# One list schedule for both feed-forwards of an attention and two-feed-forward kernel, with measured lengths and dependent operations kept apart

## The chip, the cores and the metric

The kernel runs on one core of a Trainium2 chip. The time is the device time of one execution in microseconds (us). Three runs of the kernel before took 731.81, 727.86 and 728.3 us; their median is 728.3 us. The execution that was profiled took 728.8 us, and the span that its trace covers is 726.7 us.

Five engines take part. PE (TensorE) multiplies matrices, and PEld is its loading of weights, which runs beside it. DVE (VectorE) and ACT (ScalarE) do the work between the products. POOL (GpSimd) squares one tensor of each chunk. SP issues every DMA.

## The reference

Three stages follow one another on 2304 tokens (4 sequences of 576) with 512 features:

```python
# attention, 8 heads of 64, each row sees itself and the 63 rows before it
scores = (q @ k.T) / 8, masked to 0 <= row - col < 64
x = softmax(scores) @ v                       # [2304, 512]
# feed-forward 1
h = maximum(x @ w_in, 0)                      # [2304, 2048]
x2 = (h * h) @ w_out                          # [2304, 512]
# feed-forward 2
h = x2 @ w2_in                                # [2304, 1024]
solu = h * softmax(h)                         # over the 1024
ln = (solu - mean) / sqrt(var + 1e-6) * g_ln  # over the 1024
out = ln @ w2_out                             # [2304, 512]
```

The two weight matrices of each feed-forward come as 64-bit floating point numbers.

## The kernel before, in words

**Blocks, units and passes.** The rows are cut into 36 blocks of 64. Two blocks make a unit of the attention: one call of `attention(n, rank)`, in which PE forms the scores, DVE masks them and takes the maxima, ACT takes the exponentials, POOL scales, PE transposes, ACT copies, PE multiplies with v, and ACT and DVE split the result into two parts, `x`. Feed-forward 1 runs over the blocks in five passes of 8, 6, 8, 6 and 8 blocks (`PASSES`), so of 512, 384, 512, 384 and 512 columns.

**Products in three terms.** Each product of a feed-forward is the sum of three (`TERMS`): high part by high part, high by low, low by high. A 128-row chunk of the hidden layer (`kk`, 16 in feed-forward 1) is then one group of 12 matmuls into `ps_h` (`product`, L402) and one of 12 into `ps_y` (`second`, L428). Between the two, ACT takes the relu and the square, POOL the exact square, and DVE the rest that the high part leaves (`rest`, L418).

**Weights.** `weights()` turns a 128x512 piece from 64-bit numbers into a high and a low part: ACT scales (L206), DVE shifts and masks (`bits`, L210), puts in the sign (`sign`, L215) and the low bits (`low`, L220), ACT rounds (`first`, L228) and DVE takes the rest (`second`, L231). The three DVE operations in the middle write and read one tile, `wm`. Feed-forward 1 has 32 such pieces (16 `wa`, 16 `wb`), all made in pass 0, and feed-forward 2 has 16 (`w2i`, `w2o`), made in the last pass in the room that used `wa` pieces leave. For this reason pass 0 goes twice over the chunks, with two halves of 256 columns: the second half starts `BEHIND` = 6 chunks after the first.

**The order of the work.** Attention, feed-forward 1 and the weights are tasks of a `Plan`. Each task has an engine, an expected length, a rank, its predecessors and the buffers that it takes and gives. `Plan.run` is a list scheduler: again and again it takes the task that could start first, with the lower rank where two could start at once. A result costs `HOP` = 0.12 us more if it goes to another engine and nothing if it stays. Tasks marked `port` on DVE and POOL don't overlap in the plan. The instructions are then issued in that order, and every engine works through its own list strictly in order.

**Feed-forward 2 before** is no part of the plan. It is written out by hand behind it, from L527, in 18 tiles of 128 rows: `load_x` reads x2 back from DRAM, `split_x` splits it, `mm_h` (L547) makes `ps_h` with 24 matmuls of 512 columns and then runs the softmax and the statistics on DVE and ACT, `mm_t` transposes (`ps_lt`, L587), `mm_o` makes `ps_o` with 24 matmuls and stores. Its `ps_h` uses the PSUM pair of buffers `b` that also holds the four sums `ps_y` of feed-forward 1.

Of the kernel before, what the change touches and what calls it, by code (L numbers as in the profile page):

```python
# [8 lines left out]
F32 = mybir.dt.float32  # L9
# [9 lines left out]
P = 128  # L19
# [5 lines left out]
class Plan:  # L25
# [6 lines left out]
    HOP = 0.12  # L32
# [10 lines left out]
    def run(self):  # L43
# [6 lines left out]
        while any(todo.values()):  # L50
            best = None
            for eng, ts in todo.items():
                for t in ts:
# [3 lines left out]
                    for a in t["after"]:  # L57
                        at = max(at, a["end"] + (self.HOP if a["eng"] != eng else 0.0))
# [35 lines left out]
def kernel(  # L94
# [33 lines left out]
    HALF, BEHIND = len(FIRSTS), 6  # L128
# [32 lines left out]
    x2_dram = dram.tile([P, DC, NT], F32, name="x2_dram")  # L161
# [12 lines left out]

    with ExitStack() as c1:
# [3 lines left out]
        g_p = c1.enter_context(tc.tile_pool(name="g", bufs=3))  # L179
        ps_t = c1.enter_context(tc.tile_pool(name="ps_t", bufs=2, space=PSUM))  # L180
# [9 lines left out]
        plan = Plan({"raw": RAWS, "wm": WMB, "qk": 1, "v": 1, "e": 2, "pt": 1, "t": 2, "b": 2, "a": 2, "r": 2, "g": 3})  # L190
# [5 lines left out]
        def weights(kind, i, rank, after=()):  # L196
# [37 lines left out]
            a = add("SP", 1.9, rank - 9, load, after, take=["raw"], late=2.0)  # L234
            b = add("ACT", 0.60, rank, scale, [a], take=["wm"])
            c = add("DVE", 0.37, rank, bits, [b], port=True)
            c = add("DVE", 0.62, rank, sign, [c], port=True)
            c = add("DVE", 0.62, rank, low, [c], port=True, give=["raw"])
            b = add("ACT", 0.60 + 0.66 * (kind == "2o"), rank, first, [c])
            ready[kind, i] = add("DVE", 0.62, rank, second, [b], port=True, give=["wm"])  # L240
# [6 lines left out]
        def attention(n, rank):  # L247
# [26 lines left out]
            def load_v():  # L274
                o["v"] = vt = at_p.tile([P, 2, DM], F32, tag="v", name="vt", bufs=1)
# [90 lines left out]
            qk = ["r", "r"] if n == 1 else ["qk"]  # L366
            lq = add("SP", 1.9, rank - 6, load_qk, take=qk, late=2.0)
            lv = add("SP", 1.0 * half, rank - 2, load_v, [v_after.get(n - 1)], take=["v"], late=2.0)
            v_after[n] = lv
            s = add("PE", 0.5 + 0.45 * half, rank, scores, [lq], take=["t", "t", "e"], give=qk)  # L370
            first_scores.append(s)
            ns = []
            for a in range(2):
                d = add("DVE", 0.05 + 0.3 * half, rank, lambda a=a: masked(a), [s], give=["t"])
                d = add("DVE", 0.05 + 0.3 * half, rank, lambda a=a: maximum(a), [d])
                for b in range(0, HP, HP // 2):
                    e = add("ACT", 1.0 + 0.07 * half, rank, lambda a=a, b=b: exps(a, b), [d])
                d = add("DVE", 0.32, rank, lambda a=a: inverse(a), [e])
                ns.append(add("POOL", 0.12 + 0.48 * half, rank, lambda a=a: norm(a), [d], port=True))
            p = add("PE", 0.12 + 0.43 * half, rank, transposes, [*ns, p_after.get(n - 1)], take=["t"] * half + ["pt"], give=["e"])  # L380
            c = [add("ACT", 0.58, rank, lambda a=a: copied(a), [p], give=["t"]) for a in range(half)]
            p = add("PE", 1.35, rank, values, [*c, lv], take=["b" if alone else "t"], give=["pt", "v"])
            p_after[n] = p
            h = add("ACT", 0.62, rank, high, [p] + x_free.get(t - 2, []))
            x_ready[n] = add("DVE", 0.65, rank, rest, [h], give=["b" if alone else "t"])


        acc, in_of, out_of = {}, {}, {}

        def mm(N):  # L390
            return 12 * (N / 2400 + 0.0125) + 0.05

        def ffn(t, n0, n1, kk, rank, done):
# [28 lines left out]
            def second():  # L422
                if t not in acc:
                    acc[t] = [ps_b.tile([P, 2, 512], F32, tag="b", name="ps_y") for _ in range(2)]
                for d in range(DC):
                    for n, (wi, xi) in enumerate(TERMS):

                        T.matmul(acc[t][d // 2][:, d % 2, n0:n1], wb[kk][:, wi, d * P : d * P + P], o["g"][:, xi, :N],  # L428
                                 start=kk == 0 and n == 0 and n0 == 0, stop=last and n == 2)

            i = add("PE", mm(N), rank, product, [ready["a", kk], *done], take=["a"])
# [3 lines left out]
            r = add("ACT", N / 1200 + 0.14, rank, relu, [i], take=["r"], give=["a"])  # L435
            s = add("ACT", N / 1200 + 0.16, rank, square, [r], take=["g"])
            e = add("POOL", N / 550 + 0.13, rank, exact, [s], port=True)
            e = add("DVE", N / 960 + 0.1, rank, rest, [e], port=True, give=["r"])
            first = kk == 0 and n0 == 0
            before = out_of.get((t, 0, 0)) if kk == 0 else out_of[t, n0, kk - 1]  # L440
            p = add("PE", mm(N), rank + 4.5, second, [e, ready["b", kk], before], take=["b", "b"] if first else [], give=["g"])
            out_of[t, n0, kk] = p
            if last:
                ys = []
                for d in range(DC):
                    def evict(d=d):
                        o["y", d] = y = raw_p.tile([P, 512], F32, tag="wm", name="y", bufs=WMB)
                        if d % 2:
                            S.activation(out=y[:, :n1], in_=acc[t][d // 2][:, d % 2, :n1], func=AF.Copy)  # L449
                        else:  # L450
                            V.tensor_copy(y[:, :n1], acc[t][d // 2][:, d % 2, :n1])

                    def store(d=d):
                        at = starts[t] * BLK
                        nc.sync.dma_start(out=x2_dram[:, d, at : at + n1], in_=o["y", d][:, :n1])

                    y = add("ACT" if d % 2 else "DVE", 0.62, rank, evict, [p] + ys[-1:] * (d % 2), take=["wm"], give=["b"] * (d % 2))
                    ys.append(y)
                    add("SP", 1.0, rank, store, [y], late=2.0, give=["wm"])


        PAIR0, PAIR = 13.0, 6.6
# [8 lines left out]
        for n in range(u0):  # L471
            attention(n, 2.0 + n)
        for i in range(u0):
            attention(u0 + i, begin[0] + i * (BEHIND - 1) * PAIR / u0)

        def attention_of(t):
            lo = begin[t - 1] + (BEHIND * PAIR if t == 1 else 0)
# [47 lines left out]


    with ExitStack() as c2:  # L527
        s_p = c2.enter_context(tc.tile_pool(name="s", bufs=2))
        ps_t = c2.enter_context(tc.tile_pool(name="ps_t2", bufs=2, space=PSUM))
        NTT = NT // P  # L530
        sol, lnT, rst = {}, {}, {}
        x2 = {}

        def load_x(i):
            xr = s_p.tile([P, DC, P], F32, tag="xr", name="xr")
            nc.sync.dma_start(out=xr, in_=x2_dram[:, :, i * P : i * P + P])
            x2[i] = xr

        x2s = {}

        def split_x(i):
            xr = x2.pop(i)
            xx = s_p.tile([P, 2, DC, P], F32R, tag="xx", name="xx")
            S.activation(out=xx[:, 0], in_=xr, func=AF.Copy)
            V.tensor_tensor(out=xx[:, 1], in0=xr, in1=xx[:, 0].bitcast(F32), op=ALU.subtract)
            x2s[i] = xx

        def mm_h(i):
            xx = x2s.pop(i)
            ps = ps_b.tile([P, 2, 512], F32, tag="b", name="ps_h2")  # L550
            for hf in range(NH2):
                n = 0
                for c in range(DC):
                    for wi, xi in TERMS:
                        T.matmul(ps[:, hf, :], xx[:, xi, c, :], w2i[hf * DC + c][:, wi, :],  # L555
                                 start=n == 0, stop=n == 3 * DC - 1)
                        n += 1
            h = ps.rearrange("p a b -> p (a b)")
            nmax = s_p.tile([P, 1], F32, tag="nmax2", name="nmax2")
            V.tensor_reduce(out=nmax, in_=h, axis=AX.X, op=ALU.max, negate=True)  # L560
# [12 lines left out]
            rstd = s_p.tile([P, 1], F32, tag="rstd", name="rstd", bufs=4)
            V.tensor_scalar(out=rstd, in0=mv[:, 1:2], scalar1=1e-6, scalar2=None, op0=ALU.add)  # L574
# [86 lines left out]
```

## Time and profile before

| | |
|---|---|
| median of 3 runs | 728.3 us |
| profiled execution, its span | 728.8 us, 726.7 us |
| PE busy | 697.0 us (96%) |
| PEld, DVE, ACT, POOL busy | 605.5, 371.5, 307.9, 139.0 us |
| chain that ended last | PE 81%, DVE 11%, issue 2%, DMA 2%, ACT 2% |

The busy shares are averages over stages that differ. In the first 140 us DVE makes the weights; after that PE works without a break until the end of feed-forward 1; then comes a short gap, and feed-forward 2 is again PE without a break. How the span falls into stages is read from the windows, and what ended the chain in each of them from the chain of waits.

### The profile page before, as it was taken

The numbers are of one execution on the slowest core, as the hardware profiler recorded it, in microseconds if no ns is written. First come the engines' busy times: TensorE is split into PE (matmuls) and PEld (weight loads), VectorE is DVE, ScalarE is ACT, GpSimd is POOL, SyncE is SP. The second block draws the span as 40 slices with busy tenths as digits, with TensorE's granted clock in tenths as the row PEclk, the third lists the DMA queues.
The fourth block names the chain that finished last, engine by engine and source line by source line (L and its number), as shares of the span: only waits on it lengthen the run. The fifth ranks groups of instructions, "written<-read, shape, count | busy, mean of one in ns | idle before, by whom it ended". The sixth has DMA issues, their size and how long they took to land.

```text
span 726.7 us, 11758 instructions
## 1 busy us (share of the span) xinstructions
PE 697.0 (96%) x4630; PEld 605.5 (83%) x4630; DVE 371.5 (51%) x678; ACT 307.9 (42%) x755; POOL 139.0 (19%) x161
## 2 busy tenths in 40 slices
PE   6687999999999999999999999998999999999997
PEld 3677888999999888788999988886888888888876
DVE  3999999522333221322223166555675646665561
ACT  5776767334445233433434243455323231323132
POOL 2122332412223122222222121121010011010100
PEclk9889999999999999999999999999999999999999
DMA  7766644012222211212111062222211011110001
GB/s 225 252 203 227 212 151 147 31 38 87 66 66 67 73 36 30 63 40 86 39 66 60 1 206 99 89 85 66 80 44 58 30 45 44 59 39 35 14 30 43
DMA packets 34565, 60.51 MB, mean 83 GB/s; under 512 B 5072, under 2 KB 16336, under 8 KB 34512
## 3 DMA queue, kind: packets, MB, share of 16 engines
q1 hardware_dynamic: 34512, 59.78, 24.7%
q8 instruction: 36, 0.59, 0.3%
q14 instruction: 17, 0.14, 0.1%
HBM read 50.34 MB, written 9.44 MB: 82 GB/s over the span
## 4 chain that ended last, share of the span: by engine, by line
PE 81%; DVE 11%; issue 2%; DMA 2%; ACT 2%; SPq 0%; POOL 0%; ACTq 0%; DVEq 0%
PE ps_h L402 24%; PE ps_y L428 23%; PE ps_h L555 14%; PE ps_o L599 14%; DVE wm L215 3%; PE ps_lt L587 2%; DVE wm L220 2%; PE ps_v L350 2%; PE ps_s L294 2%; PE ps_p L327 1%; DVE wm L210 1%; DVE wa L231 1%; DVE g L418 1%; DVE wb L231 1%; DMA qk<-in_k 1%
## 5 line engine op out<-in xcount | busy, mean ns | idle before, releaser
L402 PE MATMUL ps_h<-x,wa 128*128 128x256 f32 (+2 forms) x1152 | 220.5, 344 | 4.3 <-DVE wa L231 2.5
L428 PE MATMUL ps_y<-g,wb 128*128 128x256 f32 (+2 forms) x1152 | 219.6, 343 | 5.2 <-DVE g L418 5.0
L428 PEld LDWEIGHTS ps_y<-g,wb 128*128 128x128 f32 x1152 | 188.2, 190 | 26.2 <-DVE g L418 7.1
L402 PEld LDWEIGHTS ps_h<-x,wa 128*128 128x128 f32 x1152 | 190.4, 194 | 23.1 <-DVE wa L231 3.4
L415 POOL TENSOR_TENSOR r<-r 128x256 f32<-128x256 f32 (+2 forms) x96 | 84.0, 877 | 305.3 <-ACT g L412 288.3
L418 DVE TENSOR_TENSOR g<-r,g 128x256 fp32r<-128x256 f32 (+2 forms) x96 | 55.0, 580 | 152.0 <-POOL r L415 147.6
L408 ACT ACTIVATE r<-ps_h 128x256 f32<-128x256 f32 (+2 forms) x96 | 46.9, 489 | 157.6 <-PE ps_h L402 153.4
L555 PE MATMUL ps_h<-w2i,xx 128*128 128x512 f32 x432 | 104.9, 393 | 0.4 <-ACT y L449 0.4
L599 PE MATMUL ps_o<-w2o,lnT 128*128 128x512 f32 x432 | 104.5, 391 | 0.8 <-ACT lnT L588 0.5
L599 PEld LDWEIGHTS ps_o<-w2o,lnT 128*128 128x128 f32 x432 | 80.7, 188 | 17.9 <-ACT lnT L588 0.8
L555 PEld LDWEIGHTS ps_h<-w2i,xx 128*128 128x128 f32 x432 | 79.9, 188 | 17.0 <-ACT y L449 0.8
L309 ACT ACTIVATE e<-e,nmax 128x128 f32<-128x128 f32 (+1 forms) x144 | 55.0, 384 | 38.4 <-DVE nmax L305 38.4
L602 ACT ACTIVATE o<-ps_o,rstd 128x512 f32<-128x512 f32 x18 | 12.4, 689 | 111.8 <-PE ps_o L599 109.9
L575 POOL TENSOR_TENSOR rstd<-rstd,mhalf 128x1 f32<-128x1 f32 x18 | 16.8, 935 | 192.5 <-DVE rstd L574 192.5
L412 ACT ACTIVATE g<-r 128x256 fp32r<-128x256 f32 (+2 forms) x96 | 50.3, 524 | 5.1 <-PE ps_y L428 2.3
L318 POOL TENSOR_TENSOR e<-e,sums 128x512 f32<-128x512 f32 (+1 forms) x36 | 37.0, 1031 | 73.2 <-DVE sums L315 61.9
L560 DVE TENSOR_REDUCE nmax<-ps_h 128x1 f32<-128x1024 f32 x18 | 21.9, 1218 | 43.9 <-PE ps_h L555 43.9
L301 DVE SCALAR_TENSOR_TENSOR e<-ps_s,mask 128x512 f32<-128x512 f32 (+1 forms) x36 | 23.5, 653 | 38.9 <-PE ps_s L294 38.9
L589 DVE TENSOR_TENSOR lnT<-ps_lt,lnT 128x512 fp32r<-128x512 f32 x36 | 23.3, 683 | 36.3 <-ACT lnT L588 36.3
L220 DVE SCALAR_TENSOR_TENSOR wm<-wraw,wm 128x512 int32<-128x512 int32 x48 | 36.3, 757 | 1.2
L215 DVE SCALAR_TENSOR_TENSOR wm<-wraw,wm 128x512 int32<-128x512 int32 x48 | 35.1, 731 | 1.3
L206 ACT ACTIVATE wm<-wraw 128x512 f32<-128x512 f32 x48 | 31.5, 664 | 2.3 <-DMA wraw<-in_w_out 1.7
(57 smaller groups left out, 511.9 us busy)
## 6 DMA issues: line engine op xcount, KB each, us to landing
wraw<-in_w_in SPq DMA_DIRECT2D x24, 512.0 KB, 3.8
wraw<-in_w_out SPq DMA_DIRECT2D x24, 512.0 KB, 3.3
vt<-in_v SPq DMA_DIRECT2D x32, 256.0 KB, 2.9
kt<-in_k SPq DMA_DIRECT2D x16, 384.0 KB, 4.2
xr<-x_dram SPq DMA_DIRECT2D x18, 256.0 KB, 3.1
out<-o SPq DMA_DIRECT2D x18, 256.0 KB, 2.0
qt<-in_q SPq DMA_DIRECT2D x17, 256.0 KB, 2.8
x_dram<-y SPq DMA_DIRECT2D x12, 256.0 KB, 2.5
```

The lines of the kernel that those rows point to most:

```text
L215: V.scalar_tensor_tensor(out=t, in0=o["raw"][:, :, 1], scalar=-0x80000000, in1=t, op0=ALU.bitwise_and, op1=ALU.bitwise_or)
L220: V.scalar_tensor_tensor(out=t, in0=o["raw"][:, :, 0], scalar=29, in1=t, op0=ALU.logical_shift_right, op1=ALU.bitwise_or)
L309: S.activation(out=o["er"][:, a, w], in_=o["er"][:, a, w], func=AF.Exp, bias=o["nmax"][:, a, w : w + 1], accum_out=o["sums"][:, a, w : w + 1])
L318: G.tensor_tensor(out=o["er"][:, a], in0=o["er"][:, a], in1=o["sums"][:, a].unsqueeze(2).to_broadcast([P, HP, W]), op=ALU.mult)
L402: T.matmul(ps[:, :N], wa[kk][:, wi, c * P : c * P + P], xs[t][:, xi, c, n0:n1], start=n == 0, stop=n == 3 * DC - 1)
L408: S.activation(out=o["r"], in_=o["h"][:, :N], func=AF.Relu)
L412: S.activation(out=o["g"][:, 0, :N], in_=o["r"], func=AF.Square)
L415: G.tensor_tensor(out=o["r"], in0=o["r"], in1=o["r"], op=ALU.mult)
L418: V.tensor_tensor(out=o["g"][:, 1, :N], in0=o["r"], in1=o["g"][:, 0, :N].bitcast(F32), op=ALU.subtract)
L428: T.matmul(acc[t][d // 2][:, d % 2, n0:n1], wb[kk][:, wi, d * P : d * P + P], o["g"][:, xi, :N], start=kk == 0 and n == 0 and n0 == 0, sto ...
L555: T.matmul(ps[:, hf, :], xx[:, xi, c, :], w2i[hf * DC + c][:, wi, :], start=n == 0, stop=n == 3 * DC - 1)
L599: T.matmul(ps, l[:, xi, kk, :], w2o[kk][:, wi, :], start=n == 0, stop=n == 3 * KF2 - 1)
```

## The change

1. **Both feed-forwards are in the plan.** The hand-written part goes. A function `tile2` adds the steps of each tile of feed-forward 2 as tasks. The products with `w2i` are two tasks of 12 matmuls, those with `w2o` also two; the transposes of a tile are placed 6 us of rank behind its products, and the `w2o` products 1.5 tiles behind (growing to 3.9 over the last four tiles). Its working tiles lie in the room of used `wb` pieces. In the last pass the four sums `ps_y` take one buffer of the pair `b` and the two single buffers `t` of the attention, so that the other `b` is free for the first tile of feed-forward 2. x2 goes to five DRAM tensors, one for each pass, so that a read waits for its own pass alone. The last chunk's product of the last pass gets a rank 6 us earlier.
2. **Dependent operations stay apart.** A result that stays on its engine now costs `GAP` = 0.1 us on DVE and ACT, and the hop depends on the engine that gives it (0.10 to 0.35 us).
3. **Lengths.** Nearly all expected lengths are changed (a weight load from 1.9 to 1.4 us, a square on POOL of 256 columns from 0.60 to 0.62 us, two exponentials of a late unit from 1.14 to 0.77 us, and so on).
4. **Pass 0.** `BEHIND` is 2 and not 6; the ranks of the units and chunks are new. The second unit's v goes into a free `g` buffer instead of waiting for the single buffer `v`.

```diff
-    HOP = 0.12
+    HOP = {"DVE": 0.16, "ACT": 0.14, "POOL": 0.35, "PE": 0.12, "SP": 0.1}
+    GAP = {"DVE": 0.1, "ACT": 0.1}
...
-                        at = max(at, a["end"] + (self.HOP if a["eng"] != eng else 0.0))
+                        at = max(at, a["end"] + (self.HOP[a["eng"]] if a["eng"] != eng else self.GAP.get(eng, 0.0)))
...
-    HALF, BEHIND = len(FIRSTS), 6
+    HALF, BEHIND, LAST = len(FIRSTS), 2, len(PASSES) - 1
...
+                if n == 1:
+                    o["v"] = vt = g_p.tile([P, 2, NMAX], F32, tag="g", name="vt")
...
-                    acc[t] = [ps_b.tile([P, 2, 512], F32, tag="b", name="ps_y") for _ in range(2)]
+                    acc[t] = [ps_b.tile([P, 2, 512], F32, tag="b", name="ps_y") for _ in range(1 if t == LAST else 2)]
+                    acc[t] = [a[:, i] for a in acc[t] for i in range(2)]
+                    if t == LAST:
+                        acc[t] += [ps_t.tile([P, 512], F32, tag="t", name="ps_y") for _ in range(2)]
...
-        PAIR0, PAIR = 13.0, 6.6
+        PAIR0, PAIR = 14.29, 8.64
+        V0, LATER, OUT = -2.75, 40.72, 4.28
+        UNIT = (1.43, 3.36, 23.15, 34.53)
...
+            a = add("SP", 1.0, rank - 14, load_x, stored[t] + h_of.get(i - 3, []), take=["wb"], late=2.0)
+            a = add("ACT", 0.54, rank - 6, x_high, [a], take=["wb"])
+            a = add("DVE", 0.60, rank - 6, x_low, [a], port=True, give=["wb"])
+            for hf in range(NH2):
+                a = add("PE", mm(512), rank, lambda hf=hf: mm_h(hf), [a, *(ready["2i", hf * DC + c] for c in range(DC))],
+                        take=["b"] * (hf == 0), give=["wb"] * (hf == 1))
+            h_of[i] = [a]
+            a = add("DVE", 1.17, rank, max_h, [a])
+            a = add("ACT", 1.10, rank, exp_h, [a], take=["wb"])
+            a = add("DVE", 1.60, rank, solu, [a], give=["b"])
+            a = add("DVE", 1.50, rank, stats, [a])
+            r = add("POOL", 1.05, rank, root, [a])
+            a = add("DVE", 0.56, rank, centered, [a], port=True)
+            p = add("PE", 0.95, rank + 6, transposes2, [a], take=["t", "t"], give=["wb"])
...
+        NTT, TILE = NT // P, 4 * mm(512) + 1.2
+        for i in range(NTT):
+            at = begin[-1] + TILE * i
+            tile2(i, at, at + TILE * (1.5 + 0.6 * max(0, i - (NTT - 5))))
```

**DVE in pass 0.** The numbers tell the tiles apart: `wm` is the piece under work. Before:

```order
L210 TENSOR_SCALAR wm_1291<-wm_1291 128x512
L215 SCALAR_TENSOR_TENSOR wm_1291<-wraw_1245,wm_1291 128x512
L220 SCALAR_TENSOR_TENSOR wm_1291<-wraw_1245,wm_1291 128x512
L210 TENSOR_SCALAR wm_1330<-wm_1330 128x512
L215 SCALAR_TENSOR_TENSOR wm_1330<-wraw_1270,wm_1330 128x512
L220 SCALAR_TENSOR_TENSOR wm_1330<-wraw_1270,wm_1330 128x512
L231 TENSOR_TENSOR wa_1441<-wm_1291,wa_1441 128x512
```

And in the changed kernel, where L212, L217, L222, L233 and L424 are the former L210, L215, L220, L231 and L418:

```order
L217 SCALAR_TENSOR_TENSOR wm_909<-wraw_844,wm_909 128x512
L233 TENSOR_TENSOR wa_1025<-wm_881,wa_1025 128x512
L222 SCALAR_TENSOR_TENSOR wm_909<-wraw_844,wm_909 128x512
L424 TENSOR_TENSOR g_1031<-r_1029,g_1031 128x256
L217 SCALAR_TENSOR_TENSOR wm_952<-wraw_887,wm_952 128x512
L212 TENSOR_SCALAR wm_1010<-wm_1010 128x512
L233 TENSOR_TENSOR wb_1067<-wm_909,wb_1067 128x512
L222 SCALAR_TENSOR_TENSOR wm_952<-wraw_887,wm_952 128x512
L233 TENSOR_TENSOR wa_1096<-wm_952,wa_1096 128x512
```

An operation on a piece now mostly has one on another tile between itself and the operation that it needs.

**PE between the feed-forwards.** `ps_y` is feed-forward 1; `ps_h` with a number is a tile of feed-forward 2. Before:

```order
L402 MATMUL ps_h<-x,wa 128x512 x12
L428 MATMUL ps_y<-g,wb 128x512 x24
L555 MATMUL ps_h_5103<-w2i,xx 128x512 x24
L555 MATMUL ps_h_5151<-w2i,xx 128x512 x24
```

And in the changed kernel (L408, L437 and L543 are the former L402, L428 and L555):

```order
L408 MATMUL ps_h<-x,wa 128x512 x12
L437 MATMUL ps_y<-g,wb 128x512 x12
L543 MATMUL ps_h_5073<-w2i,xx 128x512 x12
L437 MATMUL ps_y<-g,wb 128x512 x12
L543 MATMUL ps_h_5073<-w2i,xx 128x512 x12
L543 MATMUL ps_h_5130<-w2i,xx 128x512 x24
L543 MATMUL ps_h_5175<-w2i,xx 128x512 x12
L581 MATMUL ps_lt<-ident,e_5146 128x128 x8
```

Half a tile of feed-forward 2 now stands ahead of the last group of feed-forward 1.

**PE within feed-forward 2.** A tile's `e` is named after its `ps_h`: e_5241 belongs to the second tile before ps_h_5396, and e_5397 to the tile directly before ps_h_5426. Before:

```order
L555 MATMUL ps_h_5396<-w2i,xx 128x512 x21
L599 MATMUL ps_o<-w2o,lnT 128x512
L555 MATMUL ps_h_5396<-w2i,xx 128x512 x2
L599 MATMUL ps_o<-w2o,lnT 128x512 x23
L587 MATMUL ps_lt<-ident,e_5241 128x128 x8
```

And in the changed kernel:

```order
L543 MATMUL ps_h_5303<-w2i,xx 128x512 x12
L596 MATMUL ps_o<-w2o,lnT 128x512 x24
L543 MATMUL ps_h_5426<-w2i,xx 128x512 x12
L581 MATMUL ps_lt<-ident,e_5397 128x128 x8
L543 MATMUL ps_h_5426<-w2i,xx 128x512 x12
```

The transposes of a tile now follow its own products after one `ps_o` and half a `ps_h`; before, two whole tiles' products stood between.

## Rows read from the trace of the kernel before

**Rows 1.** The page's first line.
```profile
span 726.7 us, 11758 instructions
```

**Rows 2.** Windows: stretch, length, busy PE, PEld, DVE, ACT, POOL, granted clock, DMA.
```profile
23.80:62.00 38.20, 30.33 (x298) 26.77 (x299) 36.80 (x70) 30.01 (x91) 9.64 (x11) 0.83 0.71 242
62.00:120.90 58.90, 52.84 (x513) 49.91 (x511) 56.52 (x102) 40.83 (x112) 17.26 (x19) 1.00 0.54 187
120.90:155.30 34.40, 34.35 (x307) 33.95 (x308) 17.32 (x30) 13.98 (x33) 10.47 (x14) 1.00 0.07 26
155.30:498.60 343.30, 343.30 (x2286) 303.30 (x2285) 120.68 (x222) 143.71 (x362) 79.70 (x84) 1.00 0.21 69
498.60:508.80 10.20, 7.59 (x25) 5.43 (x23) 5.33 (x10) 5.91 (x10) 1.04 (x1) 0.83 0.40 120
508.80:702.40 193.60, 193.58 (x914) 161.30 (x915) 114.86 (x202) 53.90 (x95) 15.91 (x17) 1.00 0.13 43
702.40:722.80 20.40, 19.63 (x96) 15.63 (x94) 7.87 (x14) 6.32 (x11) 0.92 (x1) 1.00 0.10 39
```

**Rows 3.** Chain that ended last, in order of time: start, length, what.
```profile
154.08 1.43 PE ps_y L428 x12
155.50 0.87 PE ps_p L327 x8
158.49 1.08 PE ps_v L350 x32
173.79 1.03 PE ps_s L294 x32
...
561.67 4.80 PE ps_h L555 x21
567.15 5.22 PE ps_o L599 x23
```

**Rows 4.** Timeline of DVE in pass 0: start, length, instruction.
```profile
61.56 0.41 DVE L210 TENSOR_SCALAR wm<-wm 128x512 int32<-128x512 int32 x1
62.00 0.69 DVE L215 SCALAR_TENSOR_TENSOR wm<-wraw,wm 128x512 int32<-128x512 int32 x1
62.73 0.69 DVE L220 SCALAR_TENSOR_TENSOR wm<-wraw,wm 128x512 int32<-128x512 int32 x1
63.34 0.68 DVE L364 TENSOR_TENSOR x<-ps_v,x 128x512 fp32r<-128x512 f32 x1
...
66.33 0.42 DVE L418 TENSOR_TENSOR g<-r,g 128x256 fp32r<-128x256 f32 x1
66.67 0.42 DVE L210 TENSOR_SCALAR wm<-wm 128x512 int32<-128x512 int32 x1
67.00 0.68 DVE L231 TENSOR_TENSOR wb<-wm,wb 128x512 fp32r<-128x512 f32 x1
67.60 1.10 DVE L215 SCALAR_TENSOR_TENSOR wm<-wraw,wm 128x512 int32<-128x512 int32 x1
```

**Rows 5.** Timeline of DVE: the eighth and the last of 32 finished weight pieces.
```profile
44.67 0.68 DVE L231 TENSOR_TENSOR wb<-wm,wb 128x512 fp32r<-128x512 f32 x1
...
133.62 0.69 DVE L231 TENSOR_TENSOR wb<-wm,wb 128x512 fp32r<-128x512 f32 x1 [0.36 <-ACT wb L228]
```

**Rows 6.** Timeline of PE between the feed-forwards.
```profile
504.05 4.37 PE L428 MATMUL ps_y<-g,wb 128*128 128x512 f32 x11 [2.23 <-DVE g L418]
...
508.82 16.60 PE L555 MATMUL ps_h<-w2i,xx 128*128 128x512 f32 x72 [0.40 <-ACT y L449]
```

**Rows 7.** Timeline of DVE: one tile of feed-forward 2 from maximum to centring.
```profile
573.51 1.23 DVE L560 TENSOR_REDUCE nmax<-ps_h 128x1 f32<-128x1024 f32 x1 [5.59 <-PE ps_h L555]
...
579.35 1.21 DVE L560 TENSOR_REDUCE nmax<-ps_h 128x1 f32<-128x1024 f32 x1
580.47 0.68 DVE L545 TENSOR_TENSOR xx<-xr,xx 128x512 fp32r<-128x512 f32 x1
...
581.45 0.74 DVE L576 TENSOR_SCALAR e<-e,mv 128x1024 f32<-128x1024 f32 x1
```

More of the change, by code (lines that the diff above doesn't have):

```diff
@@ L159 @@
     gcol = const.tile([P, KF2], F32, name="gcol")
-    x2_dram = dram.tile([P, DC, NT], F32, name="x2_dram")
+    x2_dram = [dram.tile([P, DC, n * BLK], F32, name=f"x2_dram{t}") for t, n in enumerate(PASSES)]
     REBIAS = 2.0**-112
@@ L232, in second @@
                 store[i] = o["d"]
-            a = add("SP", 1.9, rank - 9, load, after, take=["raw"], late=2.0)
-            b = add("ACT", 0.60, rank, scale, [a], take=["wm"])
-            c = add("DVE", 0.37, rank, bits, [b], port=True)
+            a = add("SP", 1.4, rank - 9, load, after, take=["raw"], late=2.4)
+            b = add("ACT", 0.57, rank, scale, [a], take=["wm"])
+            c = add("DVE", 0.36, rank, bits, [b], port=True)
             c = add("DVE", 0.62, rank, sign, [c], port=True)
             c = add("DVE", 0.62, rank, low, [c], port=True, give=["raw"])
-            b = add("ACT", 0.60 + 0.66 * (kind == "2o"), rank, first, [c])
-            ready[kind, i] = add("DVE", 0.62, rank, second, [b], port=True, give=["wm"])
+            b = add("ACT", 0.54 + 0.74 * (kind == "2o"), rank, first, [c])
+            ready[kind, i] = add("DVE", 0.61, rank, second, [b], port=True, give=["wm"])
         x_ready, x_free, first_scores, v_after, p_after = {}, {}, [], {}, {}
@@ L364, in rest @@
                 V.tensor_tensor(out=o["x"][1], in0=o["o"], in1=o["x"][0].bitcast(F32), op=ALU.subtract)
-            qk = ["r", "r"] if n == 1 else ["qk"]
-            lq = add("SP", 1.9, rank - 6, load_qk, take=qk, late=2.0)
-            lv = add("SP", 1.0 * half, rank - 2, load_v, [v_after.get(n - 1)], take=["v"], late=2.0)
+            qk, vs = (["r", "r"], "g") if n == 1 else (["qk"], "v")
+            lq = add("SP", 1.5, rank - 6, load_qk, take=qk, late=2.4)
+            lv = add("SP", 2.6 if alone else 1.4, rank + (V0 if alone else -2), load_v, [v_after.get(n - 1)], take=[vs], late=2.4)
             v_after[n] = lv
-            s = add("PE", 0.5 + 0.45 * half, rank, scores, [lq], take=["t", "t", "e"], give=qk)
+            s = add("PE", 0.55 + 0.3 * half, rank, scores, [lq], take=["t", "t", "e"], give=qk)
             first_scores.append(s)
@@ L434, in ffn @@
                 x_free.setdefault(t, []).append(i)
[L435 to L438, printed above, removed]
+            r = add("ACT", N / 1200 + 0.11, rank, relu, [i], take=["r"], give=["a"])
+            s = add("ACT", N / 1200 + 0.11, rank, square, [r], take=["g"])
+            e = add("POOL", N / 600 + 0.19, rank, exact, [s], port=True)
+            e = add("DVE", N / 960 + 0.07, rank, rest, [e], port=True, give=["r"])
             first = kk == 0 and n0 == 0
             before = out_of.get((t, 0, 0)) if kk == 0 else out_of[t, n0, kk - 1]
-            p = add("PE", mm(N), rank + 4.5, second, [e, ready["b", kk], before], take=["b", "b"] if first else [], give=["g"])
+            gone = ["wb"] * (t == LAST)
+            p = add("PE", mm(N), rank + OUT, second, [e, ready["b", kk], before], take=[] if not first else ["b", "t", "t"] if t == LAST else ["b", "b"],
+                    give=["g", *gone])
             out_of[t, n0, kk] = p
@@ L470 @@
         u0 = HALF // 2
[L471 to L474, printed above, removed]
+        for n, rank in enumerate(UNIT):
+            attention(n, rank)
         def attention_of(t):
-            lo = begin[t - 1] + (BEHIND * PAIR if t == 1 else 0)
+            lo = begin[t - 1] + LATER * (t == 1)
             hi = begin[t] - 10
```

214 lines of the change are left out of this document (105 added, 109 removed).

## Prediction

> **What bounds the kernel now.** I read four views, in this order. The windows by stage [rows 2] show who works without a break. From 155.3 to 498.6 us PE is busy for the whole of the 343.3 us, and from 508.8 to 702.4 us for 193.58 of 193.60: no change of order can win anything there, and it can only lose. From 23.8 to 62.0 us PE is busy for 30.3 of 38.2 us, at a granted clock of 0.83, and DVE for 36.8; from 62.0 to 120.9 us PE for 52.8 of 58.9 and DVE for 56.5. So DVE bounds the first 120 us, in which it makes the weights. From 120.9 us on PE has no idle time left, although DVE finishes its last weight piece only at 134.3 us [rows 5]: the second half of pass 0 lags six chunks and PE works off what has piled up, until the last group of pass 0 ends at 155.5 us [rows 3]. Two small losses are left: 498.6 to 508.8 us, between the feed-forwards, and the last 20.4 us.
>
> The reader is therefore to look for PE's idle time alone, since all its other time is work that stays. The span is 726.7 us [rows 1]; the profiled execution took 728.8, so 2.1 us lie around it, and it is 0.5 us above the median of 728.3. Sums are made against 728.8. About 0.5% (3.6 us) is what a measurement of this kernel can tell from no change.
>
> **Pass 0, seen from DVE.** Spacing: the start-to-start time [rows 4] is 0.44 us from `bits` to the `sign` that needs it and 0.33 us from `bits` to something unrelated, so 0.11 us is lost; 0.73 us from `sign` to its `low` and 0.60 to 0.61 behind unrelated work, so 0.13 lost. In the order of before, up to the last weight piece, 25 `sign` and 21 `low` stand directly behind what they need, and 12 maxima directly behind their mask; in the changed order 2, 3 and 6. That saves 23 x 0.11 + 18 x 0.13 + 6 x 0.11 (priced like `sign`, an estimate) = 2.5 + 2.3 + 0.7 = 5.5 us. Added ahead of the last piece: five more `rest` operations (28 for 23), 5 x 0.34 = 1.7 us, and three more mask or maximum operations at 0.60, 1.8 us. The net is 2.0 us less. Five more squares on POOL: a DVE operation under which one runs took 1.10 us instead of 0.68 [rows 4], so up to 5 x 0.42 = 2.1 us more, and nothing if they fall into DVE's gaps. I take 0.7: the last piece is ready at 134.3 - 2.0 + 0.7 = 133.0 us.
>
> Behind the last piece DVE has only four `rest` operations of pass 0 left in the new order, where nine were left before. PE then has four groups of 12 (1.43 us each), one transposition (0.87) and one product with v (1.08) [rows 3]: 7.7 us, and about 1 us until the first can start. Seen from DVE, pass 0 ends no earlier than 133.0 + 8.7 = 141.7 us.
>
> **Pass 0, seen from PE.** The second half can begin once the x of the fourth unit is split. That is at 63.3 us now [rows 4], behind 12 finished pieces. In the new order it stands behind 7. Against DVE's list up to the eighth piece of today (done at 45.3 us [rows 5]) that is four masks and maxima, two inverses, one `sign` and the split itself more, one `second` less, and a dozen places spaced: about 2 us in all, so 47.5 us. PE's order then has 57 of its 64 groups left, 57 x 1.43 = 81.5 us, and four units at 1.03 + 0.87 + 1.08 = 2.98, 11.9 us: 93.4 us of work, and an end no earlier than 140.9 us. So both engines ask for about 141 to 142 us, and that is the good end. If PE idles a tenth of the way, as from 62.0 to 120.9 us (52.84 of 58.90 [rows 2]), the end is 47.5 + 93.4/0.897 = 151.6. With only two chunks of reserve there are more waits than today, but today's tenth is DVE's bound and not PE's; I take the middle, 147. The new order has also done one unit more by then (seven scores for six, six products with v for five): 3.0 us of PE work that is not done later. Gain of pass 0: 155.5 - 147 + 3.0 = 11.5 us, between 6.9 and 16.8.
>
> The early v of the second unit, in a free `g` buffer, takes away a wait for `v` near 20 us, but PE's first product waits there for x, which stands at the same place of DVE's list; I count nothing for it, and at most 1 us either way.
>
> **Between the feed-forwards.** PE has to do two groups of 512 columns here. A matmul of that size takes 5.22/23 = 0.227 us [rows 3], so 24 take 5.4 us and would end at 498.8 + 5.4 = 504.2; feed-forward 2 starts at 508.82 [rows 6]. The loss of 4.6 us is a wait for the last `rest` (2.23), one for the eviction that frees `ps_h` (0.40), and 11 matmuls in 4.37 instead of 2.50 us, under the lowered clock (0.83 [rows 2]) that follows the idle time. In the new order 12 matmuls of the first tile (2.7 us) stand ahead of the last group, and a free buffer is kept for them; so the chain from the last product to the last group is covered for 5.4 us; it took 504.05 - 498.80 = 5.25 us with another tile's split ahead of the `rest` on DVE. All 4.6 us go. What is late next is DVE: in the first three tiles two evictions and three softmax chains fall into some 21 us, at about 7 us each (worked out with the second rival), and the third tile's transposes wait; I put 1.5 us on it (0 to 4). Net 3.1 us.
>
> **The end.** From 702.4 to 722.8 us PE does 24 transpositions of 128 columns (2.6 us at 0.87 for 8) and 72 matmuls (16.4): 19.0 of 20.4 us. In the new order three groups of `ps_o` are kept back behind the last products and cover the last softmax. I count 1.3 us.
>
> **Sum.** 728.8 - 11.5 - 3.1 - 1.3 = 712.9, so 713 us. The steps outside these places (five DRAM tensors, lengths in passes 1 to 4, weights of feed-forward 2 at another place of the last pass) cost nothing as long as PE stays covered: two to three groups of 2.7 us each stand between a product and its `ps_y`, over a chain that took at most 5.25 us. If the weight pieces of the last pass stand in that chain's way on DVE, 2 us here and there are lost; this is in the range.
>
> **The rivals.**
>
> *Pass 0 keeps its length (0.17).* DVE's sum falls by only 2.0 of some 118 us, and both engines work strictly in order: a `rest` that waits for POOL now holds back weight pieces. Today six chunks of reserve keep PE busy after 120.9 us; with two there is none. For it: the two good ends agree within 1 us, so no engine has slack. Against it: the new order is laid out with lengths close to the rows. If each of the last 16 pieces is held for 0.5 us, pass 0 ends at 155 and only the unit done ahead and the two small gains remain: 728.8 - 0.5 - 3.0 - 4.4 = 721.
>
> *Feed-forward 2 waits in every tile (0.10).* This one ends on the other side. Today two tiles' products lie between a tile's products and its transposes; in the new order 24 matmuls and 12, so 8.2 us. One tile's chain from maximum to centring took 573.51 to 582.19, 8.7 us [rows 7], of which 1.1 (the next tile's maximum) and 0.6 (another tile's split) no longer stand in it: 7.0, and with 0.6 for the one split that can still come into it and about 0.5 for PE's ends, 7.5 to 8.1. It fits by 0.1 to 0.7 us. What passes 8.2 us is paid in some 15 tiles: 0.5 us costs 7 us, and from 1.3 us on (a chain of 9.5) the whole gain is gone: 713 + 15 x 1.3 = 732, slower than before. For it: DVE is strictly in order and the splits of `lnT` stand ahead of the next maximum. Against it: DVE is busy only for 114.9 of 193.6 us there.
>
> *The gap between the feed-forwards stays (0.12).* If the first tile waits (for its x2, its weights or its buffer), the 4.6 us are not won and a clock drop may follow: 713 + 4.6 = 717.5.
>
> *Spacing gives nothing (0.03).* If a `sign` or a `low` starts no sooner behind unrelated work than behind its own input, the 5.5 us drop out of DVE's sum: the last piece comes at 138.5 us, pass 0 ends no earlier than 147.2, and with the same 5 us on top at 152.5: 713 + 5.5 = 718.5. Rows 4 speak against it.
>
> [...]
>
> **How the numbers follow.** The forecast has 0.58, with a range of its own from 707 (both good ends) to 718. The rivals have 0.42: 0.17 at 721, 0.10 at 720 to 735, 0.12 at 717.5 and 0.03 at 718.5. The range is 706 to 724: above it lie the worse half of the feed-forward 2 rival and the upper part of the first. Faster by over 0.5% (below 724.7): 0.58 + 0.12 + 0.03, 0.12 of the first rival and 0.02 of the second, 0.87. Within 0.5%: 0.05 of the first and 0.03 of the second, 0.08. Slower: 0.05.
>
> **What the profile would show.** Right: PE's last group of pass 0 ends between 143 and 151 us; `sign` and `low` take about 0.6 us from start to start; DVE's last weight piece is done near 133 us; the first `ps_h` of feed-forward 2 follows `ps_y` without a gap and without a clock drop; a tile of feed-forward 2 takes 11.8 us of PE without idle time. Wrong: PE idle behind `rest` or the weights beyond 62 us by more than a tenth; pass 0's end at 153 us or later; idle time ahead of `ps_lt` in every tile; idle time in the last pass behind `g`.

## The result, and the profile after

| | before | after |
|---|---|---|
| median (runs) | 729.93 us (4) | 705.91 us (4: 704.83 to 706.33) |
| ratio, 95% interval | | 0.967, 0.964 to 0.970 |
| profiled execution, its span | 728.8, 726.7 us | 705.88, 703.9 us |
| PE busy, PE idle in the span | 697.0, 29.7 us | 687.7, 16.2 us |

The change is worth 3.3%. The forecast was 713 us with a range of 706 to 724: the sign and the places were right, the size was too small, and the result lies just below the range. Of the 22.8 us of span, 13.5 are idle time of PE, and 9.3 are busy time: the same 4630 matmuls (the pages count as many in both traces) ran faster. Part of that is the clock: from 22.2 to 47.5 us 0.93 was granted, against 0.80 in the same stretch before; [rows 2] shows 0.83 for 23.8 to 62.0 us and again for the gap between the feed-forwards (1.00 is the upper level, 2.4 GHz; a mean below it holds time at the lower, 1.2 GHz).

The windows of the changed kernel, by its own stages (columns as in rows 2):

```profile
22.20:47.50 25.30, 20.50 (x233) 17.61 (x233) 23.86 (x48) 20.18 (x72) 7.33 (x7) 0.93 0.66 215
47.50:143.00 95.50, 95.50 (x973) 93.23 (x972) 85.87 (x165) 65.60 (x180) 33.41 (x39) 1.00 0.50 170
143.00:484.10 341.10, 341.10 (x2214) 301.43 (x2213) 116.89 (x216) 144.05 (x351) 80.65 (x82) 1.00 0.21 68
484.10:489.60 5.50, 5.50 (x25) 4.48 (x25) 3.73 (x7) 1.35 (x2) 0.22 (x1) 1.00 0.02 4
489.60:514.60 25.00, 24.62 (x122) 20.42 (x121) 19.79 (x35) 9.39 (x17) 1.65 (x3) 1.00 0.27 84
514.60:661.80 147.20, 147.20 (x698) 122.61 (x697) 83.21 (x144) 42.77 (x74) 11.26 (x12) 1.00 0.14 45
661.80:700.10 38.30, 38.20 (x180) 31.32 (x178) 20.29 (x35) 9.58 (x17) 2.39 (x3) 1.00 0.06 21
```

The second number after the stretch is PE's busy time. From 47.5 us to the end of feed-forward 1 it equals the length of the stretch: PE has no idle time at all there, where before it was busy for 52.8 of 58.9 us from 62.0 to 120.9 us [rows 2]. DVE is busy for 85.87 of 95.5 us there. Of the 16.2 us that PE still idles in the whole span, 12.0 lie ahead of 47.5 us (12.5 before), and 5.1 of these are the first scores' wait for the load of k.

DVE's idle time from 47.5 to 143 us falls into two parts, ahead of the end of its last weight piece (134.65 us) and behind it:

```profile
47.50:134.65 87.15, 87.15 (x881) 85.08 (x880) 81.80 (x155) 60.14 (x160) 29.97 (x35) 1.00 0.53 177
134.65:143.00 8.35, 8.35 (x94) 8.15 (x93) 4.07 (x12) 5.46 (x21) 3.44 (x4) 1.00 0.27 93
```

So DVE idles for 5.4 of 87.15 us (6%) while it still makes weights, and the other 4.3 us come when they are all done.

PE around the end of pass 0 and between the feed-forwards (start, length, instruction, in brackets a wait):

```profile
139.91 3.11 PE L437 MATMUL ps_y<-g,wb 128*128 128x256 f32 x24
142.86 6.43 PE L408 MATMUL ps_h<-x,wa 128*128 128x384 f32 x36
...
478.39 2.90 PE L408 MATMUL ps_h<-x,wa 128*128 128x512 f32 x12
481.13 2.96 PE L437 MATMUL ps_y<-g,wb 128*128 128x512 f32 x12
483.92 2.90 PE L543 MATMUL ps_h<-w2i,xx 128*128 128x512 f32 x12
486.66 2.96 PE L437 MATMUL ps_y<-g,wb 128*128 128x512 f32 x12
489.45 11.06 PE L543 MATMUL ps_h<-w2i,xx 128*128 128x512 f32 x48
...
513.56 1.07 PE L581 MATMUL ps_lt<-ident,e 128*128 128x128 f32 x8 [0.38 <-DVE e L573]
```

The last group of pass 0 ends at 143.0 us; the prediction took 155.5 from [rows 3] as the end before. Between the feed-forwards no wait is left of those in [rows 6]. Two rows of the kernel before, from the same view, that the prediction didn't use:

```profile
159.50 1.70 PE L428 MATMUL ps_y<-g,wb 128*128 128x256 f32 x12
...
495.89 2.90 PE L402 MATMUL ps_h<-x,wa 128*128 128x512 f32 x12
```

The first is one more group of 256 columns, so of pass 0, behind the end that the prediction took. The second is the last product of feed-forward 1, which now starts at 478.39: 17.5 us were won ahead of it. From this start on, 108 matmuls took 29.5 us before (to 508.82 + 16.60); after, 96 take 22.1, and 12 more are 2.7: 4.7 us won, less the wait of 0.38 further on. The rest, 22.8 - 17.5 - 4.3 = 1.0 us, lies behind that, in feed-forward 2 and mainly at its end: PE idled there for 0.77 us in the last 20.4 us [rows 2], and now for 0.10 in the last 38.3.

DVE in the changed kernel, in pass 0 and at the last weight piece:

```profile
41.92 0.68 DVE L217 SCALAR_TENSOR_TENSOR wm<-wraw,wm 128x512 int32<-128x512 int32 x1
42.52 0.42 DVE L424 TENSOR_TENSOR g<-r,g 128x256 fp32r<-128x256 f32 x1
42.86 0.68 DVE L222 SCALAR_TENSOR_TENSOR wm<-wraw,wm 128x512 int32<-128x512 int32 x1
...
46.73 0.69 DVE L370 TENSOR_TENSOR x<-ps_v,x 128x512 fp32r<-128x512 f32 x1
...
133.97 0.68 DVE L233 TENSOR_TENSOR wb<-wm,wb 128x512 fp32r<-128x512 f32 x1
```

A `sign` takes 0.60 us from start to start here, against 0.73 in [rows 4]. The x of the fourth unit is split from 46.73 us on (the second half was predicted to start at 47.5), against 63.34 in [rows 4]. But the last weight piece starts at 133.97, no earlier than the 133.62 of [rows 5]. DVE does not finish sooner; more of PE's work is done by the time it finishes.

### The profile page after: what moved, and what is told of

Read it like the earlier page. It is cut to its first block, busy times and chain, and to the rows that moved or that the text cites. A ratio compares the mean times of both kernels' runs of the same rounds, so it can differ in the third digit from the quotient of the medians.

```text
span 703.9 us, 11738 instructions
## 1 busy us (share of the span) xinstructions
PE 687.7 (98%) x4630; PEld 600.0 (85%) x4630; DVE 366.7 (52%) x678; ACT 307.0 (44%) x755; POOL 141.2 (20%) x161
## 4 chain that ended last, share of the span: by engine, by line
PE 93%; DVE 5%; ACT 1%; issue 1%; DMA 0%; SPq 0%; ACTq 0%
PE ps_y L437 30%; PE ps_h L408 28%; PE ps_o L596 13%; PE ps_h L543 12%; PE ps_v L356 3%; PE ps_s L300 2%; PE ps_lt L581 2%; PE ps_p L333 2%; PE ps_warm L646 1%; DVE bn L566 1%; DVE nmax L550 1%; DMA kt<-in_k 0%; DVE wm L217 0%; DVE nmax L311 0%; DVE e L561 0%
## 5 line engine op out<-in xcount | busy, mean ns | idle before, releaser
L437 PE MATMUL ps_y<-g,wb 128*128 128x256 f32 (+2 forms) x1152 | 217.5, 343 | 2.1 <-DVE g L424 2.0
L408 PE MATMUL ps_h<-x,wa 128*128 128x256 f32 (+2 forms) x1152 | 210.8, 337 | 0.7 <-DVE x L370 0.6
L437 PEld LDWEIGHTS ps_y<-g,wb 128*128 128x128 f32 x1152 | 187.2, 189 | 22.7 <-DVE g L424 2.7
L408 PEld LDWEIGHTS ps_h<-x,wa 128*128 128x128 f32 x1152 | 185.9, 189 | 17.1 <-DVE x L370 0.8
L421 POOL TENSOR_TENSOR r<-r 128x256 f32<-128x256 f32 (+2 forms) x96 | 87.1, 908 | 279.9 <-ACT g L418 274.2
L424 DVE TENSOR_TENSOR g<-r,g 128x256 fp32r<-128x256 f32 (+2 forms) x96 | 56.6, 595 | 153.1 <-POOL r L421 153.1
L543 PE MATMUL ps_h<-w2i,xx 128*128 128x512 f32 x432 | 104.9, 393 | 0.0
L596 PE MATMUL ps_o<-w2o,lnT 128*128 128x512 f32 x432 | 101.3, 390 | 0.0
L543 PEld LDWEIGHTS ps_h<-w2i,xx 128*128 128x128 f32 x432 | 80.0, 188 | 16.3
L315 ACT ACTIVATE e<-e,nmax 128x128 f32<-128x128 f32 (+1 forms) x144 | 55.0, 384 | 38.6 <-DVE nmax L311 38.3
L576 POOL TENSOR_TENSOR rstd<-rstd,mhalf 128x1 f32<-128x1 f32 x18 | 15.3, 850 | 190.3 <-DVE rstd L570 180.0
L418 ACT ACTIVATE g<-r 128x256 fp32r<-128x256 f32 (+2 forms) x96 | 50.1, 523 | 3.7 <-PE ps_y L437 1.5
L555 ACT ACTIVATE e<-ps_h,nmax 128x1024 f32<-128x1024 f32 x18 | 20.1, 1118 | 63.9 <-DVE nmax L550 60.2
L307 DVE SCALAR_TENSOR_TENSOR e<-ps_s,mask 128x512 f32<-128x512 f32 (+1 forms) x36 | 22.1, 653 | 29.9 <-PE ps_s L300 29.9
L222 DVE SCALAR_TENSOR_TENSOR wm<-wraw,wm 128x512 int32<-128x512 int32 x48 | 36.4, 766 | 0.4
L585 ACT ACTIVATE lnT<-ps_lt 128x512 fp32r<-128x512 f32 x36 | 19.5, 595 | 36.1 <-PE ps_lt L581 36.1
```

Of the source, the lines that this page charges most:

```text
L222: V.scalar_tensor_tensor(out=t, in0=o["raw"][:, :, 0], scalar=29, in1=t, op0=ALU.logical_shift_right, op1=ALU.bitwise_or)
L315: S.activation(out=o["er"][:, a, w], in_=o["er"][:, a, w], func=AF.Exp, bias=o["nmax"][:, a, w : w + 1], accum_out=o["sums"][:, a, w : w + 1])
L408: T.matmul(ps[:, :N], wa[kk][:, wi, c * P : c * P + P], xs[t][:, xi, c, n0:n1], start=n == 0, stop=n == 3 * DC - 1)
L418: S.activation(out=o["g"][:, 0, :N], in_=o["r"], func=AF.Square)
L421: G.tensor_tensor(out=o["r"], in0=o["r"], in1=o["r"], op=ALU.mult)
L424: V.tensor_tensor(out=o["g"][:, 1, :N], in0=o["r"], in1=o["g"][:, 0, :N].bitcast(F32), op=ALU.subtract)
```

## The experiments

Medians of four runs each. They were taken in three groups: the first four experiments of the table behind "changed", the next four, and the last four. The kernel before had a median of 730.2, 728.9 and 729.9 us in these groups, so about 1 us between groups is not to be read; the ratios are to the kernel before of the same group.

| kernel | median us | ratio to before, 95% | PE busy of 95.5 us (47.5 to 143) |
|---|---|---|---|
| before | 728.9 to 730.2 | 1 | 85.6 |
| changed | 705.9 | 0.967 (0.964 to 0.970) | 95.5 |
| no distance | 711.5 | 0.975 (0.974 to 0.977) | 91.9 |
| six chunks behind | 714.6 | 0.978 (0.977 to 0.980) | 89.8 |
| feed-forward 2 by hand | 715.8 | 0.981 (0.980 to 0.982) | 94.8 |
| old pass 0 | 724.9 | 0.993 (0.992 to 0.995) | 85.1 |
| changed, no low bits | 705.3 | 0.967 (0.965 to 0.969) | 95.5 |
| before, no low bits | 718.3 | 0.984 (0.982 to 0.986) | 93.0 |
| changed, two terms | 704.5 | 0.965 (0.963 to 0.967) | 78.2 |
| no distance, six behind | 718.7 | 0.986 (0.984 to 0.987) | 88.3 |
| changed, both left out | 691.5 | 0.949 (0.945 to 0.952) | 84.5 |
| three chunks behind | 713.8 | 0.978 (0.976 to 0.980) | 90.5 |
| distance 0.14 | 706.6 | 0.969 (0.967 to 0.972) | 94.2 |
| q and k earlier | 705.7 | 0.968 (0.966 to 0.970) | 94.4 |

**No distance between dependent operations.**

```diff
-    GAP = {"DVE": 0.1, "ACT": 0.1}
+    GAP = {}
```

> The changed kernel, except that the plan asks for no distance between dependent operations of one engine (GAP empty). Theory: from 47.5 us on TensorE is what bounds pass 0, and VectorE has about 10 us of slack until its last piece; so without the distance VectorE is up to 5.5 us later, and pass 0 ends only 0 to 3 us later: 706 to 709 us. Rival: VectorE sets the end of pass 0, as the prediction had it from both sides: the 5.5 us come back in full, 711.5 us.

711.49 us: the rival's number, and the theory with which I began fell. Windows and pieces of DVE's timeline (the traced execution took 713.19 us, 1.7 above the median, so times in it are up to that much too late):

```profile
22.20:47.50 25.30, 19.32 (x216) 16.90 (x215) 23.08 (x46) 19.38 (x65) 6.49 (x7) 0.87 0.64 209
47.50:143.00 95.50, 91.91 (x894) 87.28 (x894) 85.42 (x161) 65.57 (x181) 31.91 (x36) 1.00 0.50 164
```

```profile
63.40 0.68 DVE L217 SCALAR_TENSOR_TENSOR wm<-wraw,wm 128x512 int32<-128x512 int32 x1
64.12 0.69 DVE L222 SCALAR_TENSOR_TENSOR wm<-wraw,wm 128x512 int32<-128x512 int32 x1
64.72 0.58 DVE L320 TENSOR_SCALAR sums<-sums 128x4 f32<-128x4 f32 x1
...
141.95 1.32 DVE L233 TENSOR_TENSOR wb<-wm,wb 128x512 fp32r<-128x512 f32 x1
```

`sign` to `low` is back at 0.72 us, `low` to the unrelated next one stays at 0.60. The last weight piece is ready at 143.3 us, 8.6 later than in the changed kernel, and the first group behind pass 0 starts at 150.98 and not 142.86. DVE is busy for 85.4 of 95.5 us, as with distances, yet PE waits for it. The 10 us of slack that the theory reckoned with were not there: 4.3 of them lie behind the last piece, and the 5.4 ahead of it were not used up; there are 10.1 of them here. The edit empties the distance for the whole plan and for ACT too, so it lays out a new order; that all of the loss is the 0.12 us behind a dependent operation is not shown.

**Six chunks behind.**

```diff
-    HALF, BEHIND, LAST = len(FIRSTS), 2, len(PASSES) - 1
+    HALF, BEHIND, LAST = len(FIRSTS), 6, len(PASSES) - 1
```

> The changed kernel with the second half of pass 0 six chunks behind the first, not two. Theory: what lets TensorE work without a break from 47.5 us on is that the second half comes in early and doubles the products that each finished weight piece feeds; with six chunks TensorE idles again between 47 and about 75 us and the idle time isn't given back: 713 to 717 us. Rival: the lengths, the ranks and the spacing fill TensorE, not the distance of the halves: under 2 us later, 706 to 708 us.

714.61 us, as the theory had it, and at its place: PE waits 4.19 us in one piece for a `rest`, out of 5.7 us of idle time from 47.5 us on.

```profile
62.38 0.39 PE L437 MATMUL ps_y<-g,wb 128*128 128x256 f32 x1
66.95 2.72 PE L437 MATMUL ps_y<-g,wb 128*128 128x256 f32 x11 [4.19 <-DVE g L424]
```

**Feed-forward 2 by hand.** The tasks of `tile2` go, the hand-written part stands behind the plan again, and `LAST = -1`.

> The changed kernel, except that feed-forward 2 is written by hand behind the plan as before, and the last pass has its sums in the pair of buffers as before. Theory: the gap between the feed-forwards comes back (4.4 to 4.6 us), and 0.8 us in feed-forward 2 and at the end: 711 us. Rival: the planned feed-forward 2 is worth more, because the whole last pass is laid out with it, or nothing, because the gap has another cause: 714 us or more, or 707 us or less.

715.83 us, 9.9 more, where 5 were expected: the rival's 714 us or more. PE (the last line is cut off by the window):

```profile
481.91 2.90 PE L408 MATMUL ps_h<-x,wa 128*128 128x512 f32 x12
486.21 0.50 PE L437 MATMUL ps_y<-g,wb 128*128 128x512 f32 x1 [1.41 <-ACT g L418]
490.15 5.06 PE L437 MATMUL ps_y<-g,wb 128*128 128x512 f32 x11 [3.44 <-DVE g L424]
495.01 5.16 PE L570 MATMUL ps_h<-w2i,xx 128*128 128x512 f32 x20
```

With `LAST = -1` the last product also lost its earlier rank, so only one group stands behind it and the whole chain to `rest` is open: 4.85 us of waits, and 11 matmuls in 4.86 us (to 495.01), not 2.5. That is 7.2 of the 9.9 us; another 0.7 is idle time of PE in pass 0 (94.8 of 95.5). This run undid two things at once; for the worth of the planned feed-forward 2 the next one is the better witness.

**Old pass 0, both feed-forwards in the plan.** Lengths, hops, ranks, distances, `BEHIND` and v as before.

> The changed kernel with pass 0 as before: old lengths, hops, no distance, six chunks, old ranks, v as before; both feed-forwards stay in the plan. Theory: the parts add up, and only the 4.4 us between the feed-forwards and the 0.8 us behind are won: 723 to 724.5 us. Rival: the plan of feed-forward 2 changes the last pass too, so that the parts don't add: 720 us or less, or 727 us or more.

724.91 us against 730.21 in the same group: 5.3 us, against 5.2 expected; the theory's window of 723 to 724.5, just missed, was reckoned from a kernel before at 728.8. So both feed-forwards in the plan are worth 5.3 us, and the rest of the change, which is made for pass 0, 19.0. By the traces the last product of feed-forward 1 starts at 497.08 us here, 18.7 later than in the changed kernel, and in the kernel before 17.5 later.

**One engine relieved, then the other, then both.** In the first two kernels, made from the changed one and from the one before, the low bits of the 32 weight pieces of feed-forward 1 are left out; in the third, made from the changed one, the third term of pass 0's products; in the last both. All else keeps its place in the order.

```diff
             def low():
+                if kind in "ab":
+                    return
```

```diff
+                terms = TERMS[: 3 - (t == 0)]
                 for c in range(DC):
-                    for wi, xi in TERMS:
+                    for wi, xi in terms:
```

> The changed kernel without the step that puts the low bits into the weights of feed-forward 1 (L222 for these 32 pieces); everything else stays in its place. It takes 30 operations at 0.60 us, 18 us, off VectorE in pass 0, and nothing off TensorE. Theory 1, both engines stand at their limit from 47.5 us on: TensorE has no idle time there to give back, and only what it idles before (some 5 us) can be won: 700 to 704 us. Theory 2, VectorE alone sets the length of pass 0, as the run without distances suggests: most of the 18 us come off, 688 to 693 us.

> The kernel before without the same step. Theory 1 and theory 2 agree here that VectorE bounds the first 120 us, so that TensorE's 14 us of idle time there and some of the lowered clock come back: 711 to 718 us. Rival: the weights wait for their loads or for ScalarE, and VectorE is only busy beside that: 725 us or more.

> The changed kernel with two of the three terms in the products of pass 0 (8 matmuls in a group, not 12): a third of TensorE's work on these groups is left out, 30 us, and nothing of VectorE's. Theory 1, both engines stand at their limit: VectorE's last weight piece comes at 131 to 134 us as before, a few groups stand behind it, and 1 to 5 us are won: 701 to 705 us. Theory 2, TensorE alone is the bound from 47.5 us on, and VectorE's 10 us of idle time there are real slack: the idle time is used, and 694 to 698 us come out.

> The changed kernel with both taken away: no low bits in the weights of feed-forward 1 (18 us off VectorE) and two of three terms in the products of pass 0 (30 us off TensorE). Each alone won 0.6 and 1.5 us. Theory 1, the two engines stand at their limit together: with both relieved pass 0 gets shorter by most of the 18 us, 687 to 694 us. Rival: a third thing sets the length of pass 0 (the loads of the weights, ScalarE, or the way from a product over ScalarE, GpSimd and VectorE to its second product), and neither engine: 700 us or more.

705.32, 718.34, 704.45 and 691.45 us. Windows of pass 0 for the changed kernel without low bits, and from PE's timeline its first group behind pass 0:

```profile
47.50:143.00 95.50, 95.50 (x976) 93.43 (x975) 70.35 (x143) 64.89 (x182) 31.54 (x39) 1.00 0.51 171
```

```profile
142.73 6.43 PE L410 MATMUL ps_h<-x,wa 128*128 128x384 f32 x36
```

With two terms, the same two views and between them what PE waited for from 47.5 to 143 us (total, times, longest):

```profile
47.50:143.00 95.50, 78.15 (x759) 71.56 (x759) 88.86 (x168) 67.12 (x184) 33.94 (x39) 0.98 0.52 172
```

```profile
PE ps_y L438 <- DVE g L425: 15.6, 16, 2.4
```

```profile
141.77 6.43 PE L409 MATMUL ps_h<-x,wa 128*128 128x384 f32 x36
```

And with both left out:

```profile
47.50:143.00 95.50, 84.48 (x784) 79.00 (x783) 72.44 (x139) 66.47 (x184) 33.28 (x42) 1.00 0.54 176
```

```profile
129.61 6.43 PE L411 MATMUL ps_h<-x,wa 128*128 128x384 f32 x36
```

18 us off DVE alone leave it idle for 25 us and end pass 0 at 142.7; 30 us off PE alone leave it waiting, 15.6 us of it for `rest`, and end it at 141.8. Both together end it at 129.6. Theory 1 is shown: in the changed kernel the two engines stand at their limit together, and when one is relieved the other still holds the end. With two terms DVE's last piece is ready at 135.6 us, no earlier than in the changed kernel, although PE has time to spare. The rival, a third thing that holds pass 0 so that 700 us or more remain, is refuted.

Two numbers of theory 1 missed by a little: the changed kernel without low bits is 1.3 us above its 700 to 704, since none of PE's idle time ahead of 47.5 us came back, and the kernel before without them 0.3 above its 711 to 718. The same 18 us were worth 10.6 in that kernel, where DVE was the limit; that it was not more fits with PE, which is then nearly full (93.0 of 95.5). With both relieved neither engine is full from 47.5 us to the last piece at 123.5 (PE 65.3 and DVE 65.9 of 76.0 us); what holds pass 0 then is open.

**No distance and six behind.** Both edits from above.

> The changed kernel without distances and with the second half six chunks behind, so that new lengths, ranks and the early v are what is left of the change in pass 0. Theory: the two parts add, 5.6 and 8.7 us, since each fills another place (the distance all along, the early second half from 47 to 80 us): 719 to 722 us. Rival: both fill the same idle time, and the sum is less: 714 to 717 us.

718.74 us, a little under the theory's range and outside the rival's: 12.8 us over the changed kernel, against 5.6 + 8.7 = 14.3. These come from different groups; taken from the kernel before of the same group each time, it is 13.8 against 5.3 + 8.4 = 13.7. They add, as far as 1 us can be read. What is left of the 19.0 us, 5 to 6, goes with the lengths, the ranks and the early v, which no run takes apart.

**Three chunks behind.** `BEHIND` 3.

> The changed kernel with the second half three chunks behind, not two. If TensorE's 93 us from 47.5 us on are the bound, a chunk more of reserve brings nothing there and delays the second half by one chunk: 705 to 708 us. If two chunks are too little reserve, it is faster: 703 us or less.

713.76 us: both expectations missed by far. PE has its waits further on than with six:

```profile
80.00:110.00 30.00, 28.29 (x296) 26.68 (x295) 26.74 (x49) 19.86 (x51) 11.14 (x11) 1.00 0.64 205
110.00:143.00 33.00, 29.70 (x273) 28.23 (x274) 28.21 (x51) 20.15 (x64) 13.31 (x14) 0.95 0.25 83
```

So the 8.7 us of the run with six chunks are not shown to be the price of the distance alone: the ranks were set for two, and three with these ranks costs nearly as much (7.9 us) at another place. What three or six with ranks of their own would cost stays open.

**Two small ones.** `GAP` 0.14, and the loads of q and k at `rank - 10` instead of `rank - 6`.

> The changed kernel with a distance of 0.14 us instead of 0.10 (the traces show 0.11 to 0.13 us lost behind a dependent operation). The order of pass 0 changes in a dozen places; TensorE is without idle time already, so nothing should come of it: 705 to 707 us. If the plan's lengths have to be exact to keep both engines busy, a few us either way.

> The changed kernel with the loads of q and k 4 us of rank earlier, ahead of one or two weight pieces. What TensorE still loses lies before 47.5 us, and part of it is a wait of the scores for k. If that is what holds the fourth unit's x back, the second half begins up to 2 us earlier: 703 to 705 us. If the weight pieces that now come later are what holds it: 707 to 710 us.

706.62 and 705.68 us, no difference that can be told. The first was expected; the second lies in neither range, so what holds up PE ahead of 47.5 us stays open. No version that did all the work was faster than the changed kernel by more than can be told.

## Why the prediction was too cautious

- **Pass 0, 11.5 us predicted, 17.5 found.** The step that failed is "With only two chunks of reserve there are more waits than today [...] I take the middle, 147". PE had no wait at all from 47.5 us to the end of pass 0, and that end came at 143.0, 4.0 us earlier than put down. The two good ends, 141.7 from DVE and 140.9 from PE, were 1.3 and 2.1 us too early. On PE's side the count was exact (57 groups and four units) and the price too low: they took 95.5 us and not 93.4, without a wait. On DVE's side two errors partly cancelled: the last piece came 1.6 us later than predicted, and PE ended 8.4 us behind it, not 8.7. Of the rest of the 6.0 us, 1.6 is the group at 159.50, which I overlooked when I took 155.5 as the end of pass 0; 0.4 us is not accounted for.
- **That both engines ask for the same end** was read correctly, and is shown by the three kernels with one or both relieved. I drew the wrong conclusion from it, that no slack means waits; this order had none on PE, though the orders without distances or with three or six chunks had 3.6 to 5.7 us of idle time there. After the result I erred the other way and took DVE's idle 10 us for slack; the run without distances refuted that.
- **Spacing.** 5.5 us on DVE predicted; the run without it loses 5.6. That the two agree so closely is in part luck: the prediction's 5.5 us were an amount of DVE's time, of which it saw only 1.3 reach the last piece, and the run measures a whole new order. The rival that spacing gives nothing is refuted. The Trainium skill ("VectorE: DVE Perf Modes", section "Rules for kernel authors") advises, for chained operations, to make their number small rather than that of the semaphores. The trace agrees on the number: 32 operations fewer won 10.6 us in the kernel before. That row says nothing of the order: the kernels before and after issue the same 678 operations on DVE, and the order alone makes 0.72 to 0.73 us of a `sign` or 0.60.
- **The last weight piece, 133.0 predicted,** is ready at 134.65 (134.31 before). The prediction had already counted the added `rest`, mask and maximum operations, so they don't explain the 1.6 us. Up to the last piece DVE was busy for 118.7 us (117.8 before) and idle for 16.0 (16.5 before); which term of its sum was off is open.
- **Between the feed-forwards, 3.1 net predicted, 4.3 found.** The gap went in full. The third tile's wait was 0.38 us, not 1.5.
- **The end, 1.3 predicted, 1.0 found.** [Rows 2] have only 0.77 us of idle time there; the prediction's 19.0 us of work were priced too low against the 19.63 that they show.
- **Rivals.** Feed-forward 2 does not wait in every tile: from 514.6 to 661.8 us PE is busy for 147.20 of 147.20 us. Pass 0 did not keep its length, and the gap did not stay.

The errors, 6.0 + 1.2 - 0.3 = 6.9 us, cover the 7.1 between forecast and median but for 0.2.

## What to carry to other kernels

When two estimates of a stage's end, one from each engine's work, agree, the end can lie near them. Here it did, by 2.1 us, in an order that had been laid out with measured lengths; changes of that order (no distances, three chunks for two) put waits back and cost 5.6 and 7.9 us, so neither a margin for waits nor none can be taken for granted before the order is run.

Before idle time of an engine that works strictly in order is called slack, look where it lies. Of the 9.6 us that DVE idled here, 4.3 came when its last weight piece was done, and the 5.4 ahead of it gave nothing back when DVE's order got worse. To learn what bounds a stage, relieve each engine alone and then both: here 18 us off one engine won 0.6 us, 30 us off the other 1.5, and both together 14.5.

## What was not expected of the hardware

Nothing of the chip itself came out other than its rows said. Two numbers may help. A 128x512 operation on DVE directly behind one that it needs starts 0.72 us after it (`sign` to `low`), and 0.60 behind another. And where PE was left to wait (two terms), the granted clock from 22.2 to 47.5 us was 0.82, against 0.93 in the changed kernel, with PE busy for 17.5 instead of 20.5 us. The busy time of such a stretch alone doesn't tell the clock: with a distance of 0.14 PE was busy for 18.8 us of the same stretch, at 1.00.
